# Ten-row loads of an attention backward: other queues, another order, another place

## The chip, the cores and the metric

The kernel runs on one core of a Trainium2 chip. The metric is device time in microseconds (us). Three timed runs of the kernel before gave 902.4, 907.96 and 909.31 us; their median is 907.96. All profile lines come from one profiled execution of the same kernel, which took 901.73 us.

A core has five engines, each working through its own instructions in order: TensorE (PE in the profile, its weight loads PEld), VectorE (DVE), ScalarE (ACT), GpSimd (POOL) and SyncE (SP). In the code they are `T`, `V`, `A`, `G` and `SY`. Any of the last three may issue DMA transfers; the transfers themselves are carried out by 16 DMA engines of the core.

## The reference

The reference is a forward and backward pass of one transformer layer on 2048 rows of 512 elements in bf16, with 32 heads of 16 elements. The layer normalizes, applies a dilated local attention, adds the residual, normalizes again, applies an MLP with 1792 hidden units and gelu, and adds the residual. The outputs are the layer's result and the gradients of x, wqkv, wo, w1, b1, w2 and b2.

The attention looks at eight rows for each row, two apart:

```python
idx = pos[:, None] - off[None, :]          # off = 0, 2, 4, ..., 14
kg = k[:, :, idx_c, :]; vg = v[:, :, idx_c, :]
attn = softmax(where(mask, einsum("bhsd,bhswd->bhsw", q, kg) * scale, -1e9))
o = einsum("bhsw,bhswd->bhsd", attn, vg)
```

The backward of this attention needs three banded sums, one for each of dq, dk and dv: each row of the result is a sum over eight neighbouring rows (of k, of q, and of the gradient of o), each row weighted per head. Those neighbouring rows are what this change loads in another way.

## The kernel before, in words

The program has three stages. The first, to about 250 us, is the attention forward; the second, to about 460 us, is the MLP forward and most of its backward; the third is the attention backward with the weight gradients. q, k, v and the gradient of o (`go_d`) lie in HBM as rows of 512, in `q_d`, `k_d`, `v_d` and `go_d`.

The third stage walks over four chunks of 512 rows, in rounds `for c in range(NC + 2)` (line 869). A round first computes the attention's logit gradients of chunk c (products `pr` on VectorE at line 877 of `got` and the v window `vw`, summed on TensorE at line 883). It then does six bands of 256 rows: two for dv of chunk c-1 (kind "v"), two for dq of chunk c ("q"), two for dk of chunk c-1 ("k"). The rows of the gradient of the input of chunk c-2 (`gln1`, with TensorE's line 845, ScalarE's `gyr` at line 208, GpSimd's `c0` at line 210, VectorE's lines 216 to 221) run beside the logit gradients. So round 1 has bands v0, q1, k0, round 2 has v1, q2, k1, and round 3 has v2, q3, k2; round 0 has only q0, round 4 only v3 and k3.

A band works on a tile R of 128 partitions x 10 rows x 512 elements. Four DMAs (`w4` = 0 to 3, lines 766 to 769) each fill 32 partitions of it. A partition gets ten consecutive rows, 10,240 bytes in one piece; partitions are eight rows apart. R comes from `go_d` for v, from `k_d` for q and from `q_d` for k. VectorE multiplies four rows of R at a time with the coefficients `cf` (line 780, four products for a band), TensorE sums over partitions (line 788), ScalarE copies the result out (line 790), and GpSimd stores it to HBM (line 793).

There are three buffers for R. `load_R` takes the next band of the list `bands`, so two tiles are loaded ahead; at the start of a band (line 774) it asks for the tile two bands later, whose buffer is the one that the previous band has just finished with.

The order of every engine's instructions in this stage is the order in which the Python code issues them (`tc.manual_schedule()`, line 608). `later` puts a piece of work on a list and `slot` runs what is due: with 1 it runs in the very next slot. `slot` then fills TensorE's time with matmuls of the weight gradients from the generator `wgrads`. This filler also issues, on SyncE, the transposing loads `gwm` (line 627) of 256 x 2048 elements, which wait until TensorE has finished with one of two buffers, and the 2 MB loads `gout_r` and `ln2_r` (line 622); its results are copied by ScalarE into `gwst` (line 617) and stored by GpSimd (line 618). SyncE also issues `vw` (line 859), the four-part shifted coefficients `sh` (line 830), `ln1r` (line 175) and the stores of `go_d` (line 238), for which it waits on ScalarE's copy into `tmst` (line 236). Whatever of the filler is left after the bands runs at the end (line 981).

In the built program the DMAs that SyncE and ScalarE issue take turns on eight semaphores, and those of GpSimd on eight others. A DMA therefore waits until the eighth one before it in its group has landed.

Of the kernel before, what the change touches and what calls it, by code (L numbers as in the profile page):

```python
# [27 lines left out]
def _ap(apobj, dims, off=0):  # L28
    return bass.AP(tensor=apobj.tensor, offset=apobj.offset + off, ap=[list(d) for d in dims])
# [7 lines left out]
def kernel(  # L37
# [21 lines left out]
    V, A, T, G, SY = nc.vector, nc.scalar, nc.tensor, nc.gpsimd, nc.sync  # L59
# [4 lines left out]
    S, D = xf.shape  # L64
# [35 lines left out]
    def Y(name):  # L100
        return psY.tile([P, 512], F32, name=name, tag="y")
# [184 lines left out]
    def natural(ps):  # L286
        return ps[:].rearrange("p (d h) -> p h d", h=H)
# [424 lines left out]
    def filler(us):  # L712
        fs["debt"] += us
        while fs["debt"] > 0 and not fs["done"]:
            if fs["gate"] is not None:
                if fs["gate"] not in open_gates:
                    fs["debt"] = 0.0
                    return
                fs["gate"] = None
            x = next(fill, None)  # L720
            if x is None:
                fs["done"] = True
            elif isinstance(x, str):
                fs["gate"] = x
            else:
                fs["debt"] -= x
# [5 lines left out]
    def later(n, cost, fn):  # L732
        pend.append([n, cost, fn])

    def slot(dve_us):
        pe = 0.0
        for x in list(pend):
            x[0] -= 1
            if x[0] <= 0:
                pend.remove(x)  # L740
                x[2]()
                pe += x[1]
        filler(dve_us * RATIO - pe)
# [14 lines left out]
    def load_R():  # L758
        if rpos[0] >= len(bands):
            return  # L760
        kind, c, sc = bands[rpos[0]]
        rpos[0] += 1
        d_t = dict(v=go_d, q=k_d, k=q_d)[kind]
        row0 = c * CH + sc * 256 + (PAD if kind == "q" else 0)
        R = p3.tile([P, 10, 512], BF16, name="R", tag="rows", bufs=3)
        for w4 in range(4):
            r = row0 + (-4 * w4 - 2 if kind == "q" else 4 * w4)
            SY.dma_start(out=R[32 * w4:32 * w4 + 32].rearrange("p a d -> p (a d)"),  # L768
                         in_=_ap(d_t[r:r + 1, :], [[8 * D, 32], [1, 10 * D]]))
        rq.append(R)  # L770

    def band_tile(kind, c, sc, m, cf, gs, sca, after):
        if m == 0:
            load_R()
            bt["R"] = rq.pop(0)
        R = bt["R"]
        pr = p3.tile([P, 2, 4, 512], BF16, name="prb", tag="prod", bufs=3)
        for hf in range(2):
            o = (2 - 2 * hf if kind == "q" else 2 * hf) + 4 * m
            V.tensor_tensor(out=pr[:, hf].rearrange("p j (d h) -> p j d h", h=H),  # L780
                            in0=R[:, o:o + 4, :].rearrange("p j (d h) -> p j d h", h=H),
                            in1=cf[:, hf, sc, 4 * m:4 * m + 4].unsqueeze(2).to_broadcast([P, 4, DH, H]), op=ALU.mult)

        def pe():
            ps = Y("ps_band")
            for hf in range(2):
                for j in range(4):
                    T.matmul(ps[32 * j:32 * j + 32, :], lhsT=S32[:], rhs=pr[:, hf, j, :],  # L788
                             start=(hf == 0), stop=(hf == 1), skip_group_check=True)
            A.activation(out=gs[:, m, :].rearrange("p (h d) -> p h d", d=DH), in_=natural(ps), func=ACT.Copy, scale=sca)  # L790
            if m == 1:
                sel = dict(q=0, k=1, v=2)[kind]
                G.dma_start(out=g3_d[sel][:, 4 * c + 2 * sc:4 * c + 2 * sc + 2, :], in_=gs[:])
                if after:
                    later(1, 1.0, after)
        later(1, 0.7, pe)
        slot(2.45)

    bt = {}
    st3 = [dict() for _ in range(NC + 2)]  # L800
# [62 lines left out]
    load_ln1(0)  # L863
    p3_go(0)
    load_R()
    for _ in range(6):
        slot(0.0)
    load_R()
    for c in range(NC + 2):
        if c >= 2:  # L870
# [39 lines left out]
        def vtile(k):  # L910
            sc, m = k // 2, k % 2
            if m == 0:
                bt["gs"] = p3.tile([P, 2, 512], BF16, name="gks", tag="gks", bufs=2)
            gs = bt["gs"]
            band_tile("v", c - 1, sc, m, cfv, gs, 1.0,
                      lambda gs=gs, sc=sc, c=c: unperm(gs[:], gqkv[c - 1][:, 8:12, :], 4, sc * 256))
# [31 lines left out]
        if c < NC:  # L948
            st3[c]["sh"] = shift(c, attn)
            gqs[c] = []  # L950
            for k in range(4):
                sc, m = k // 2, k % 2
                if m == 0:
                    gqs[c].append(p3.tile([P, 2, 512], BF16, name="gqs", tag="gqs", bufs=2))
                band_tile("q", c, sc, m, cfq, gqs[c][sc], scale, None)
            if c == NC - 1:
                later(2, 0.0, lambda: open_gates.add("q"))
        if c > 0:
            cfk = coefs(p3, shk[:, 0, 0:1], 0, 512)
            for k in range(4):  # L960
                sc, m = k // 2, k % 2
                if m == 0:
                    bt["gs"] = p3.tile([P, 2, 512], BF16, name="gks", tag="gks", bufs=2)
                gs = bt["gs"]
                band_tile("k", c - 1, sc, m, cfk, gs, scale,
                          lambda gs=gs, sc=sc, c=c: unperm(gs[:], gqkv[c - 1][:, 4:8, :], 4, sc * 256))
            if c == NC:
                slot(0.5)
                slot(0.5)
                open_gates.add("k")  # L970
# [49 lines left out]
```

## Time and profile before

| | us |
|---|---|
| median of the timed runs | 907.96 |
| profiled execution | 901.73 |
| its span, first to last instruction | 899.9 |
| PE busy | 659.8 (73%) |
| DVE busy | 531.7 (59%) |
| ACT busy | 335.2 (37%) |
| POOL busy | 126.3 (14%) |
| VectorE's band products, line 780: 96 of 1.219 us | 110.8 |
| time from issue to landing of one of R's DMAs: shortest, middle, longest | 3.7, 7.5, 17.4 |

Of the DMA traffic, 116.55 MB went through the queues of SyncE and ScalarE and 28.87 MB through GpSimd's. Between 500 and 720 us the 16 DMA engines' packets took 84 to 114% of their time (packets overlap, so the share can pass 100%).

The profile names an instruction by its line, engine, operation and tiles as out<-in. Where it gives idle time, the name after the arrow is what ended the wait. A DMA's name, as R<-q_d, says what it writes and reads. "SPq" and "ACTq" are an engine's sequencer, which waits and issues; the time of a DMA line on SPq is that of its issue, not of its transfer.

### The profile page before, as it was taken

To read this page: it belongs to the slowest core of one execution; us is meant where nothing else is said; L and a number is where in the kernel's file an instruction comes from. 1 tells how busy PE (TensorE), PEld (TensorE's weight loads), DVE (VectorE), ACT (ScalarE), POOL (GpSimd) and SP (SyncE) were. 2 spreads that over 40 slices of the span, in tenths; PEclk is the share of its full clock that TensorE was granted. 3 is DMA by queue.
4 is the path that set the end of the run, shared out by engine and by line. 5 is a ranking of instruction groups with operands and counts; after the bars stand their busy time and mean duration, and the time that the engine had idled before them with its cause. 6 is when DMAs were issued, how large, how long until landed. Compare 5 with 4: busy or idle time off the path is not lost. (4 is left out here: it accounts for less than half of the span.)

```text
span 899.9 us, 10402 instructions
## 1 busy us (share of the span) xinstructions
PE 659.8 (73%) x3890; PEld 303.7 (34%) x3948; DVE 531.7 (59%) x774; ACT 335.2 (37%) x497; POOL 126.3 (14%) x213
## 2 busy tenths in 40 slices
PE   4785874655688989988975479779777597862585
PEld 2333332322233433333432133333323356731232
DVE  6786685545876868669476877957965751000000
ACT  2664754436643535634033143343323331110011
POOL 3202112120000201001010002111211122210010
PEclk9996988767899999999996579988986799987798
DMA  8645566584213223324399999999999845532351
GB/s 303 227 114 153 132 184 159 144 188 121 70 60 123 93 89 92 105 71 141 103 243 255 231 241 248 226 222 251 215 233 283 203 139 129 127 111 87 133 201 40
DMA packets 152514, 146.09 MB, mean 162 GB/s; under 512 B 96126, under 2 KB 140751, under 8 KB 147599
## 3 DMA queue, kind: packets, MB, share of 16 engines
q1 hardware_dynamic: 142942, 116.55, 51.5%
q0 software_dynamic: 9520, 28.87, 9.9%
q8 instruction: 31, 0.51, 0.3%
q14 instruction: 21, 0.16, 0.1%
HBM read 72.95 MB, written 47.80 MB: 134 GB/s over the span
## 5 line engine op out<-in xcount | busy, mean ns | idle before, releaser
L780 DVE TENSOR_TENSOR prb<-R,cf 128x2048 bf16<-128x2048 bf16 x96 | 110.8, 1219 | 28.4 <-DMA R<-q_d 22.2
L509 PE MATMUL ps_h<-ln2T,w 128*128 128x512 bf16 x222 | 61.8, 402 | 25.6 <-ACT x L512 22.3
L788 PE MATMUL ps_band<-prb,S 128*32 128x512 bf16 x384 | 42.7, 473 | 48.2 <-DVE prb L780 47.2
L698 PE MATMUL ps_gwq<-gqh,ln_r 128*128 128x512 bf16 x188 | 43.3, 387 | 30.6 <-DMA gqh<-gq_d 26.0
L557 PE MATMUL ps_gg<-goT,w2T 128*128 128x512 bf16 x218 | 53.8, 378 | 11.4 <-DVE gb1p L560 8.6
L661 PE MATMUL ps_gw<-gwm,ln_r 128*128 128x256 bf16 x448 | 54.1, 280 | 8.9 <-ACT gwst L617 8.9
L640 PE MATMUL ps_gw<-gout_r,gwm 128*128 128x512 bf16 x212 | 57.3, 411 | 1.8 <-issue 1.7
L511 ACT ACTIVATE xb<-ps_h,b1c 128x512 bf16<-128x512 f32 x56 | 38.2, 685 | 44.3 <-PE ps_h L509 42.5
L544 PE MATMUL ps_f<-w,gt 128*128 128x512 bf16 x217 | 53.0, 381 | 1.3 <-DVE gt L521 0.9
L618 POOL DMA_DIRECT2D out_dram<-gwst x58 | 31.4, 542 | 150.1 <-ACT gwst L617 143.2
L340 PE MATMUL ps_qkv<-ln1T,wqkv 128*128 128x512 bf16 x185 | 47.3, 392 | 6.8 <-ACT kt L342 3.2
L208 ACT ACTIVATE gyr<-ps_gl,rstd 128x512 bf16<-128x512 f32 x32 | 21.9, 686 | 77.0 <-PE ps_gl L570 24.1
L661 PEld LDWEIGHTS <-ln_r 128*128 128x128 bf16 x448 | 44.1, 100 | 19.0 <-issue 12.9
L790 ACT ACTIVATE gks<-ps_band 128x512 bf16<-128x512 f32 x32 | 19.0, 601 | 69.3 <-PE ps_band L788 57.7
L845 PE MATMUL ps_gl<-wqkvT,gqkvT 128*128 128x512 bf16 x188 | 44.5, 390 | 0.3 <-issue 0.2
L210 POOL TENSOR_SCALAR c<-sg 128x1 f32<-128x1 f32 x32 | 21.9, 686 | 159.8 <-ACT gyr L208 159.6
L509 PEld LDWEIGHTS <-w 128*128 128x128 bf16 x224 | 22.5, 101 | 58.9 <-issue 40.3
L277 DVE TENSOR_TENSOR prb<-R,cf 128x2048 bf16<-128x2048 bf16 x32 | 37.0, 1214 | 7.3 <-DMA R<-v_d 7.3
L512 ACT ACTIVATE x<-ps_h,b1c 128x512 bf16<-128x512 f32 x56 | 37.9, 685 | 7.9 <-DMA ln_d<-ln 5.4
L877 DVE TENSOR_TENSOR pr<-got,vw 128x4096 bf16<-128x4096 bf16 x16 | 35.9, 2285 | 8.1 <-DMA vw<-vf_d 8.1
L243 DVE TENSOR_TENSOR pr<-qt,kt 128x4096 bf16<-128x4096 bf16 x16 | 36.0, 2283 | 7.0 <-ACT qt L342 3.5
L617 ACT ACTIVATE gwst<-ps_gw 128x256 bf16<-128x256 f32 (+1 forms) x42 | 19.1, 455 | 56.1 <-DMA out_dram<-gwst 37.4
(320 smaller groups left out, 1129.0 us busy)
## 6 DMA issues: line engine op xcount, KB each, us to landing
R<-v_d SPq DMA_DIRECT2D x32, 320.0 KB, 5.4
R<-k_d SPq DMA_DIRECT2D x32, 320.0 KB, 7.9
R<-go_d SPq DMA_DIRECT2D x32, 320.0 KB, 7.5
R<-q_d SPq DMA_DIRECT2D x32, 320.0 KB, 7.3
g_d<-gt SPq DMA_DIRECT2D x12, 512.0 KB, 3.3
ln_d<-ln POOLq DMA_DIRECT2D x8, 512.0 KB, 5.7
out_dram<-gwst POOLq DMA_DIRECT2D x30, 128.0 KB, 4.2
w<-in_B_w_dram POOLq DMA_DIRECT2D x2, 1792.0 KB, 11.1
```

Source lines behind the costliest of these rows:

```text
L340: T.matmul(ps[:, gg, :], lhsT=wqkv[:, dc, sel * D + g * P:sel * D + (g + 1) * P], rhs=st_[c]["ln1T"][:, dc, :], start=(dc == 0), stop=(dc ...
L509: T.matmul(ps[:, i, :], lhsT=w1[:, dc, f * P:(f + 1) * P], rhs=ln2T[c][:, dc, :], start=(dc == 0), stop=(dc == DC - 1))
L511: A.activation(out=xb[:, f - f0, :], in_=ps[:, i, :], func=ACT.Identity, bias=b1c[:, f:f + 1])
L512: A.activation(out=x2[:, f - f0, :], in_=ps[:, i, :], func=ACT.Square, bias=b1c[:, f:f + 1])
L544: T.matmul(ps[:], lhsT=gts[f // 4][:, f % 4, j * P:(j + 1) * P], rhs=w2[:, f, :], start=(f == 0), stop=False)
L557: T.matmul(ps[:, i, :], lhsT=w2T[:, dc, f * P:(f + 1) * P], rhs=goT[:, dc, :], start=(dc == 0), stop=(dc == DC - 1))
L640: T.matmul(ps[:], lhsT=gtm[:, t, (f % 2) * P:(f % 2 + 1) * P], rhs=r16[:, t, :], start=(t == 0), stop=(t == NT - 1))
L661: T.matmul(ps[:, 0:256], lhsT=r16[:, t, dc * P:(dc + 1) * P], rhs=ghm[:, t, :], start=(t == 0), stop=(t == NT - 1))
L698: T.matmul(pss[dd][:], lhsT=r16[:, i * HN + t, dc * P:(dc + 1) * P], rhs=hv[i][:, t, :], start=(i == 0 and t == 0), stop=(i == 1 and t == ...
L780: V.tensor_tensor(out=pr[:, hf].rearrange("p j (d h) -> p j d h", h=H), in0=R[:, o:o + 4, :].rearrange("p j (d h) -> p j d h", h=H), in1=c ...
L788: T.matmul(ps[32 * j:32 * j + 32, :], lhsT=S32[:], rhs=pr[:, hf, j, :], start=(hf == 0), stop=(hf == 1), skip_group_check=True)
L845: T.matmul(ps[:], lhsT=gqkv[c][:, b, j * P:(j + 1) * P], rhs=wqkvT[:, b, :], start=(b == 0), stop=(b == 11))
```

## The change

Three things change in `load_R` and one in where it is called. The four DMAs of a tile are issued in the order 0, 2, 1, 3, so that partitions of the lower and the upper half alternate. The q tiles are issued by GpSimd, and their source is described with three dimensions of which the outermost has 8 entries, in place of two with 32 (the same rows to the same places). Of a v tile, parts 0 and 2 stay with SyncE and parts 1 and 3 are issued by ScalarE. The k tiles stay with SyncE. Lastly, `load_R` is called at the end of a band, after its second slot, and no longer at its start; it loads the same tile, two bands ahead, into the same buffer.

```diff
         R = p3.tile([P, 10, 512], BF16, name="R", tag="rows", bufs=3)
-        for w4 in range(4):
+        for w4 in (0, 2, 1, 3):
             r = row0 + (-4 * w4 - 2 if kind == "q" else 4 * w4)
-            SY.dma_start(out=R[32 * w4:32 * w4 + 32].rearrange("p a d -> p (a d)"),
-                         in_=_ap(d_t[r:r + 1, :], [[8 * D, 32], [1, 10 * D]]))
+            dst = R[32 * w4:32 * w4 + 32].rearrange("p a d -> p (a d)")
+            base = d_t[r:r + 1, :]
+            if kind == "q":
+                G.dma_start(out=dst, in_=_ap(base, [[32 * D, 8], [8 * D, 4], [1, 10 * D]]))
+            else:
+                (A if kind == "v" and w4 % 2 else SY).dma_start(out=dst, in_=_ap(base, [[8 * D, 32], [1, 10 * D]]))
         rq.append(R)
 
     def band_tile(kind, c, sc, m, cf, gs, sca, after):
         if m == 0:
-            load_R()
             bt["R"] = rq.pop(0)
@@
         later(1, 0.7, pe)
         slot(2.45)
+        if m == 1:
+            load_R()
```

In the order of the instructions this means: a q tile stands on GpSimd behind the store of the band that has just ended (line 793), a k tile on SyncE behind whatever the two slots of that band have put there, and ScalarE's half of a v tile behind the copies of that band.

## The prediction

> **What bounds the kernel now.** I read the shares and slices first, then the stage table of the attention backward (DVE's bands run from 481 to 730 us), then the waits of VectorE in that stage, then SyncE's and ScalarE's timelines around the longest waits. The waits of VectorE between 480 and 780 us:
>
> ```profile
> DVE junk L216 <- ACT gyr L208: 27.2, 13, 7.9
> DVE prb L780 <- DMA R<-q_d: 22.2, 7, 8.6
> DVE pr L877 <- DMA vw<-vf_d: 7.0, 1, 7.0
> DVE prb L780 <- DMA R<-k_d: 5.7, 3, 3.6
> DVE gx L221 <- DMA out_dram<-gx: 4.1, 1, 4.1
> ```
>
> Columns: total, times, longest. A band costs VectorE 4.63 us (four products of 1.219 us). It waits 27.9 us in all for the ten-row tiles R, none of it for those from go_d, and 7.0 us once for vw. TensorE in the same stage waits for VectorE's products (47.2 us), so both follow the loads. After the bands comes a tail of weight gradients, from about 750 to 890 us, in which no R is loaded; it moves as a block.
>
> SyncE's timeline shows what stands ahead of the late loads (start, length, line, tile):
>
> ```profile
> 469.95 1.93 SPq L768 DMA_DIRECT2D R<-k_d  x4
> 471.92 0.42 SPq L622 DMA_DIRECT2D gout_r<-in_grad_out_dram  x1
> 472.45 20.06 SPq L627 DMA_TRANSPOSE gwm<-g_d  x2
> 492.61 0.55 SPq L859 DMA_DIRECT2D vw<-vf_d  x1
> ...
> 589.60 5.41 SPq L627 DMA_TRANSPOSE gwm<-g_d  x1
> 595.05 2.53 SPq L830 DMA_DIRECT2D sh<-attn  x4
> ...
> 670.05 11.70 SPq L627 DMA_TRANSPOSE gwm<-gh_d  x1
> ```
>
> and VectorE's the two worst waits:
>
> ```profile
> 606.95 4.63 DVE L780 TENSOR_TENSOR prb<-R,cf 128x2048 bf16<-128x2048 bf16 x4 [8.60 <-DMA R<-q_d]
> ...
> 674.47 4.63 DVE L780 TENSOR_TENSOR prb<-R,cf 128x2048 bf16<-128x2048 bf16 x4 [7.37 <-DMA R<-q_d]
> ```
>
> Everything is issued by one engine in order: R for the second q band and gout_r stand ahead of two transposes, and these ahead of vw, which lands at 497.3 us although VectorE is free at 490.5. The first k band of rounds 2 and 3 of the loop waits behind a transpose and four shifts. In the packet records, R's 10,240-byte packets take 0.70 us each, two per DMA engine and DMA; the four DMAs of one R land 1.5 us apart, 6 us a tile, longer than the band that uses it.
>
> **What the Trainium skill says.** "SBUF — State Buffer", section "Can I just issue two DMAs to hit both halves?", says no: one DMA on partition 0 and one on 64 gained only 6% together. The trace agrees: the landing of the third R DMA (first one in the upper half) comes 1.5 us after the second, as within a half. "DMA: Bandwidth & Descriptors", section "Why a DMA increments its semaphore by 16 and not by 1", says that the slowest dimensions of both sides decide how many engines share a DMA, and that from GpSimd a DMA on fewer than 16 takes consecutive engines from a moving cursor. With outer dimension 8 that is eight engines of four rows each, and the next DMA (the other half) the other eight. No DMA before is of that kind. "SBUF — State Buffer", section "Who interferes with whom", expects tensor_tensor not to hold up GpSimd's descriptor writing; the trace agrees as far as it goes: GpSimd's stores take 0.54 us to issue while VectorE multiplies.
>
> **The change part by part**, against the profiled execution (901.73 us, span 899.9); the three timed runs have their median 6.2 us higher, at 907.96, and I apply the difference to that.
>
> *Order 0, 2, 1, 3.* For the k tiles, still on SyncE alone, I take 0 by the 1.5 us spacing above. Below zero at most: full overlap would halve 6 us a tile, 3 us for each late k band. For v, half on ScalarE's queue, any gain is hidden: those tiles have some 20 us of slack.
>
> *q tiles to GpSimd.* Eight tiles x 4 issues x 0.54 us = 17 us of GpSimd, which is 14% busy. If two DMAs run on two groups of engines, a tile takes about 1.5 us of latency and 2 x 1.5 us, 4.5 us from the first issue; if they don't, 7.5. The first two tiles leave SyncE: gout_r is issued 2.0 us earlier and has no R ahead in the rings (R's packets fill 471 to 477.3 us, gout_r's bulk runs 477 to 484). So gout_r, both transposes and vw come about 6.5 us earlier, vw at 490.8 instead of 497.3: **-6.5 us**, with nothing else late there (got is done at 480, products' buffers at 491). If this cover fails (gout_r slower for another reason), the gain is 0.
> The later q tiles now stand behind GpSimd's store of the preceding band, and in rounds 2 and 3 behind a weight-gradient store too (590.55 and 658.40 us). The second q tile of those rounds is then issued at 591.1 and 658.9 and lands 4.5 to 7.5 later; VectorE is ready at 590.8 and 659.4, so waits of 1.05 and 1.08 us become 4 to 8. That is hidden, since the k band after it starts only when its own R lands, at 606.8 and 674.4, and 6.7 us of work stand between. In round 1 the q wait of 3.58 stays (-1 to +1.5): 0.
>
> *k tiles, moved to the band's end.* The buffer is released as before; what counts is what they are moved past on SyncE. The first k tile of rounds 2 and 3 keeps its place (transpose, shifts, tile) but has no q tile in the rings ahead of the transpose, whose landing was 8.7 us against 6.7 in the quiet end of the stage: about -0.75 each, **-1.5 us**. Second k tile of round 1: moved past the go_d stores (534.8 and 535.7 us), lands near 543.7, as before (VectorE started at 544.1): 0. Second k tile of round 3: moved past the transpose of 670.05. Issue near 675 and transfer behind the transpose, landing near 683 instead of 680; the wait of 1.28 grows by **+3.5 us** (0 to +6).
> The gradient rows that follow absorb part: VectorE waits 4.11 us there for an out_dram<-gx store slowed by the 2 MB load of ln2_r and R of the next chunk; a later start meets a quieter DMA. **-2 us** (0 to -4).
>
> *Half the v tiles to ScalarE.* 16 issues x 0.42 us = 6.7 us on an engine about a third busy in this stage (86 of 260 us from 500 to 760), but in order with its evictions. In the built program SyncE's and ScalarE's DMAs share eight semaphores in turn, so each waits for the eighth before it to land (SyncE shows 11 such waits, 11.3 us, at L768 now). Thus ScalarE's last v load of rounds 1 and 2 waits for a gwm transpose, and that of round 3 for ln2_r. Behind it are queued an unpermuting copy and gyr, for which VectorE waits:
>
> ```profile
> 552.70 0.60 ACT L617 ACTIVATE gwst<-ps_gw 128x512 bf16<-128x512 f32 x1 [1.49 <-PE ps_gw L640]
> ...
> 555.91 0.69 ACT L208 ACTIVATE gyr<-ps_gl,rstd 128x512 bf16<-128x512 f32 x1 [1.58 <-PE ps_gl L845]
> ```
>
> ScalarE arrives at 553.3; with 0.9 us of issues and a 1.0 us copy behind, gyr is delayed only if the transpose lands after 554.0. Issued at 547.45 into emptier rings it lands at 554.4 to 556, so gyr slips by 0.4 to 2 us, while TensorE is busy without a break from 553 to 573 and sets the pace of the rows. I take 0 (0 to +20 over the three rounds, below).
>
> Sum: -6.5 - 1.5 + 3.5 - 2 = **-6.5 us**: 895.2 on the profiled execution, 901.5 against the median.
>
> **The rivals.**
> *The loads really speed up.* Two engine groups and a third queue relieve the rings, transposes too, and the R waits go by half: -14 with the -6.5, 887.5 us; all of 27.9 would be 873.6. For it: DMA share is about 1.0 from 500 to 720 us. Against it: the late tiles are k tiles, 22.2 of the 27.9 us, and these keep SyncE, the same engines and the transpose ahead.
> *ScalarE is held (slower).* If the awaited transfers land as late as before (the transpose of 547.45 at 559.27, 11.8 after issue; the one of 615.2 near 627; ln2_r at 700.39), gyr comes 1.9 us after each: 561.2, 628.9, 702.3 instead of 555.9, 624.8, 691.8: +5.3 + 4.1 + 10.5 = +20, less 6.5: 921.5 us. It decides from a landing past 554.0. For it: stores issued on this stage take up to 10 us to land. Against: the v tiles that stood ahead of these transposes no longer do.
> *Nothing moves.* The 6.5 us are won at 490 us and lost at the second k tile and on gyr: 908 us. The change then does in its place what it says, off the path.
>
> **How the numbers follow.** Forecast 0.45 (901.5, spread 895 to 907), speed-up 0.17 (880 to 894), held ScalarE 0.22 (914 to 928), nothing 0.16 (904 to 913). One per cent, about what a measurement of this kernel tells from no change, is 9.1 us: below 898.9 lie the speed-up and four tenths of the forecast, 0.35; above 917 most of the held ScalarE and a little unknown, 0.24; between, 0.41. Leaving out the fast third of the speed-up and the slow half of the held case gives 886 to 922.
>
> **What would show it.** Right: no wait of L877 for vw near 490 us; a wait of 4 to 8 us for R<-k_d in the second q band of rounds 2 and 3, and a smaller one for R<-q_d after it; R<-k_d landing within some 5 us of its first issue. Wrong: gyr's waits growing beyond 27.2 us with ScalarE idle behind a DMA (the third case); R<-q_d waits below 10 us (the speed-up); vw still late; or GpSimd's issues for R much longer than 0.54 us, which would make every q band late.

## The result and the profile after

The changed kernel takes 942.26 us (median of 4 runs, 935.25 to 950.32) against 906.74 for the kernel before on the same chip: a ratio of 1.0371, with an interval from 1.0291 to 1.0451. It is slower by some 35 us; the forecast was 901.5. Ratios leave out executions over 1.5% above the fastest of their kernel, here the profiled one (at the same granted clock as the others, 0.864 against 0.862 to 0.869) and later two of four with the call at the band's start again. The profiled execution took 950.32 us (span 948.5), 8 us over the median, so I use its trace for places and the medians for sizes.

The waits of VectorE between 480 and 820 us of the kernel after (total, times, longest):

```profile
DVE junk L216 <- ACT gyr L208: 39.6, 14, 12.9
DVE prb L783 <- DMA R<-k_d: 38.4, 5, 13.1
DVE prb L783 <- DMA R<-q_d: 22.5, 4, 11.6
```

R<-k_d, the q tiles, went from 5.7 to 38.4 us. R<-q_d stayed where it was in its sum (22.2), but other bands wait now. The wait for gyr is 12 us longer. And TensorE, in the same stretch, has a wait that it did not have before, the second line here:

```profile
PE ps_band L791 <- DVE prb L783: 74.7, 43, 11.5
...
PE ps_gw L640 <- DMA gwm<-g_d: 9.4, 1, 9.4
```

VectorE's timeline shows which bands wait:

```profile
602.14 4.63 DVE L783 TENSOR_TENSOR prb<-R,cf 128x2048 bf16<-128x2048 bf16 x4 [4.63 <-DMA R<-k_d]
614.72 4.63 DVE L783 TENSOR_TENSOR prb<-R,cf 128x2048 bf16<-128x2048 bf16 x4 [7.95 <-DMA R<-k_d]
...
630.87 1.23 DVE L783 TENSOR_TENSOR prb<-R,cf 128x2048 bf16<-128x2048 bf16 x1 [4.50 <-DMA R<-q_d]
...
689.02 4.63 DVE L783 TENSOR_TENSOR prb<-R,cf 128x2048 bf16<-128x2048 bf16 x4 [4.14 <-DMA R<-k_d]
706.79 4.63 DVE L783 TENSOR_TENSOR prb<-R,cf 128x2048 bf16<-128x2048 bf16 x4 [13.14 <-DMA R<-k_d]
...
729.68 3.50 DVE L783 TENSOR_TENSOR prb<-R,cf 128x2048 bf16<-128x2048 bf16 x3 [11.63 <-DMA R<-q_d]
```

602 and 614 are the first and second q band of round 2, 631 its second k band; 689, 707 and 730 are the same three bands of round 3. Two causes stand behind these lines. The first is on GpSimd's timeline:

```profile
591.17 0.54 POOL L796 DMA_DIRECT2D gv_d<-gks  x1 [3.37 <-ACT gks L793]
591.79 1.98 POOL L771 DMA_DIRECT2D R<-k_d  x4
600.12 0.56 POOL L796 DMA_DIRECT2D gv_d<-gks  x1 [6.35 <-ACT gks L793]
601.33 0.55 POOL L618 DMA_DIRECT2D out_dram<-gwst  x1 [0.66 <-ACT gwst L617]
602.00 1.98 POOL L771 DMA_DIRECT2D R<-k_d  x4
```

Each q tile stands behind the store of the band at whose end it is asked for, and that store waits for ScalarE's copy of TensorE's sums. The tile used at 602 is issued at 591.79, that used at 614.7 at 602.00. That is 5.7 and 4.8 us before VectorE is ready for them, at 597.5 and 606.8. In the kernel before, SyncE issued the same two tiles 14.7 and 8.5 us before VectorE was ready, at 586.1 and 590.7:

```profile
571.41 1.99 SPq L768 DMA_DIRECT2D R<-k_d  x4
...
582.22 1.97 SPq L768 DMA_DIRECT2D R<-k_d  x4
```

The second cause is on SyncE's timeline after the change:

```profile
628.58 13.60 SPq L627 DMA_TRANSPOSE gwm<-g_d  x1
642.40 11.60 SPq L773 DMA_DIRECT2D R<-go_d  x4
```

The transposing load of this step, the fourth of the seven that SyncE issues from 540 to 722 us, took 7.9 us to issue before; here it takes 13.6, and lands at 657.9, 29.3 us after its issue (the longest of before was 17.5, behind gout_r; from 540 to 720 us it was 11.8, of those whose landing the trace holds; the last packets of the two others came 10.6 and 13.3 us after issue). During that time ScalarE's halves of two v tiles, issued at 629.02 and 638.45, are in flight. The stretch from 632 to 656 us has a DMA share of 1.16 and moves 118 GB/s: the engines look full and carry about half of what they carried in this stretch before (214 GB/s at a share of 0.94).

### The profile page after: what moved, and what is told of

The parts are those of the page before. It is cut to its first block, busy times and chain, and to the rows that moved or that the text cites. A ratio compares the mean times of both kernels' runs of the same rounds, so it can differ in the third digit from the quotient of the medians.

```text
span 948.5 us, 10511 instructions
## 1 busy us (share of the span) xinstructions
PE 678.8 (72%) x3948; PEld 307.7 (32%) x3948; DVE 532.2 (56%) x774; ACT 335.9 (35%) x497; POOL 142.6 (15%) x245
## 5 line engine op out<-in xcount | busy, mean ns | idle before, releaser
L783 DVE TENSOR_TENSOR prb<-R,cf 128x2048 bf16<-128x2048 bf16 x96 | 111.0, 1219 | 66.1 <-DMA R<-k_d 38.4
L791 PE MATMUL ps_band<-prb,S 128*32 128x512 bf16 x384 | 45.4, 481 | 75.4 <-DVE prb L783 74.7
L509 PE MATMUL ps_h<-ln2T,w 128*128 128x512 bf16 x224 | 64.2, 415 | 23.5 <-ACT x L512 20.4
L640 PE MATMUL ps_gw<-gout_r,gwm 128*128 128x512 bf16 x224 | 63.6, 426 | 9.4 <-DMA gwm<-g_d 9.4
L698 PE MATMUL ps_gwq<-gqh,ln_r 128*128 128x512 bf16 x192 | 44.1, 391 | 30.1 <-DMA gqh<-gq_d 26.0
L850 PE MATMUL ps_gl<-wqkvT,gqkvT 128*128 128x512 bf16 x192 | 46.2, 399 | 0.0
L791 PEld LDWEIGHTS <-S 128*32 128x32 bf16 x384 | 10.0, 98 | 103.8 <-DVE prb L783 68.1
## 6 DMA issues: line engine op xcount, KB each, us to landing
R<-go_d ACTq DMA_DIRECT2D x16, 320.0 KB, 10.4
```

The source lines that it names most:

```text
L509: T.matmul(ps[:, i, :], lhsT=w1[:, dc, f * P:(f + 1) * P], rhs=ln2T[c][:, dc, :], start=(dc == 0), stop=(dc == DC - 1))
L640: T.matmul(ps[:], lhsT=gtm[:, t, (f % 2) * P:(f % 2 + 1) * P], rhs=r16[:, t, :], start=(t == 0), stop=(t == NT - 1))
L698: T.matmul(pss[dd][:], lhsT=r16[:, i * HN + t, dc * P:(dc + 1) * P], rhs=hv[i][:, t, :], start=(i == 0 and t == 0), stop=(i == 1 and t == ...
L850: T.matmul(ps[:], lhsT=gqkv[c][:, b, j * P:(j + 1) * P], rhs=wqkvT[:, b, :], start=(b == 0), stop=(b == 11))
```

## The experiments

Four theories go into the expectations. Theory 1: a transposing load crawls while R's packets run in another engine's queue. Theory 2: a q tile is late because it stands behind the store of the same band on GpSimd. Theory 3: the late call puts tiles behind SyncE's transposes and stores. Theory 4, the slower rival of the prediction: ScalarE is held by its own DMA issues, which wait for a semaphore. Every ratio is to the kernel before, timed on the same chip; the experiments ran on four chips, so compare ratios and not us between them, except where both kernels of a pair ran on one chip.

### One part at a time

The order alone, in the kernel before:

```diff
-        for w4 in range(4):
+        for w4 in (0, 2, 1, 3):
```

> The kernel before with only the order 0, 2, 1, 3 of the four DMAs, all still on SyncE, at the band's start. No theory gives this a part in the 35 us: 907 us, within 4 us of before; the four DMAs of a tile land 1.4 to 1.5 us apart, as they do now, halves or not. If the halves did help, the waits for R<-q_d fall below 15 us.

Measured: 900.3 us, ratio 0.9929 (0.9904 to 0.9954). A miss for all theories, and the fastest kernel of the study that leaves nothing out: it beats both. In the packet records the median time of R's 10,240-byte packets falls from 761 to 702 ns, and the middle spacing between the landings of a tile's DMAs from 1.52 to 1.45 us (v) and 1.54 to 1.41 (q); for the k tiles it stays at 1.42. The waits for R<-q_d go only from 22.2 to 20.5 us; the gain of 3.7 us at the last band is a little here and there.

The late call alone, in the old order, all on SyncE:

```diff
         if m == 0:
-            load_R()
             bt["R"] = rq.pop(0)
@@
         slot(2.45)
+        if m == 1:
+            load_R()
```

> The kernel before with only the call of load_R moved to the band's end, all on SyncE. Theory 1 (transposes and R's packets on different queues slow each other down): everything is still in one queue, so within 5 us of before. Theory 3 (the later place puts tiles behind SyncE's transposes and stores): +8 to +15 us, with waits for R<-k_d in the second q band and for R<-q_d in the second k band.

Measured: 924.5 us, ratio 1.0206 (1.0163 to 1.0249). Theory 3 holds, a little over its range. VectorE's waits for tiles in this kernel, 450 to 800 us:

```profile
DVE prb L785 <- DMA R<-k_d: 28.8, 3, 13.3
DVE prb L785 <- DMA R<-q_d: 23.2, 6, 8.6
```

The first q tile of each round still comes in time (it lands 0.9 to 1.8 us before the band ahead of it ends), the second lands 12.9 and 13.2 us after that point in rounds 2 and 3, and the second k tiles 5.2 to 8.6 us after. Those are behind what the band's second slot has put on SyncE.

The q tiles alone on GpSimd, asked for at the band's start as before:

```diff
-            SY.dma_start(out=R[32 * w4:32 * w4 + 32].rearrange("p a d -> p (a d)"), ...)
+            if kind == "q":
+                G.dma_start(out=dst, in_=_ap(base, [[32 * D, 8], [8 * D, 4], [1, 10 * D]]))
+            else:
+                SY.dma_start(out=dst, in_=_ap(base, [[8 * D, 32], [1, 10 * D]]))
```

> The kernel before with only the q tiles on GpSimd (outer dimension 8, order 0, 2, 1, 3), asked for at the band's start as before. Theory 1 (two queues slow each other down): +10 to +20 us, gwm landing over 12 us after issue where GpSimd's R tiles are in flight. Theory 2 (a q tile is late because it is asked for behind the store of the band just ended): asked for a band earlier in GpSimd's order, it has 5 us more; R<-k_d waits fall to under 15 us from 38, and the time is within 5 us of before or faster by up to 6 (vw comes earlier).

Measured: 903.2 us, ratio 0.9968 (0.9951 to 0.9984); this contains the new order, so GpSimd itself costs some 0.4% on 0.9929. The waits for R<-k_d are 3.5 us in all. GpSimd as the issuer isn't what hurts: theory 2's second half. Theory 1 expected 10 to 20 us here and missed. The packet records show why this run hardly tests it: of the 1,024 R packets in GpSimd's queue only 7 start within 1 us of a hundred or more of a transpose's packets. In the next kernel it is 164 of the 512 in ScalarE's queue.

Parts 1 and 3 of the v tiles alone on ScalarE, at the band's start:

```diff
-            SY.dma_start(out=R[32 * w4:32 * w4 + 32].rearrange("p a d -> p (a d)"), ...)
+            (A if kind == "v" and w4 % 2 else SY).dma_start(out=dst, in_=_ap(base, [[8 * D, 32], [1, 10 * D]]))
```

> The kernel before with only parts 1 and 3 of the v tiles on ScalarE (order 0, 2, 1, 3), asked for at the band's start. Theory 1 (two queues slow each other down): +10 to +20 us, gwm landing some 20 us or more after issue in one of the rounds, TensorE waiting for it at L640. Theory 4 (ScalarE is held by its own DMA issues that wait for a semaphore): about the same sum, but with gwm landing as before and gyr late because ScalarE stands idle before the issue of R<-go_d. Theories 2 and 3: within 4 us of before.

Measured: 935.6 us, ratio 1.0336 (1.0309 to 1.0362), with the new order: +35 us on 900.3, where theory 1 had expected 10 to 20. SyncE's timeline of the order alone, and then of this kernel, at the same step of round 1:

```profile
544.40 6.26 SPq L627 DMA_TRANSPOSE gwm<-g_d  x1
550.77 1.91 SPq L773 DMA_DIRECT2D R<-go_d  x4
563.23 4.42 SPq L627 DMA_TRANSPOSE gwm<-g_d  x1
567.75 0.61 SPq L865 DMA_DIRECT2D vw<-vf_d  x1
```

```profile
546.87 22.06 SPq L627 DMA_TRANSPOSE gwm<-g_d  x1
569.03 1.42 SPq L773 DMA_DIRECT2D R<-go_d  x2
570.54 11.67 SPq L627 DMA_TRANSPOSE gwm<-g_d  x1
582.31 0.61 SPq L865 DMA_DIRECT2D vw<-vf_d  x1
```

SyncE is held in the transpose for 22 us instead of 6, and everything behind it, the other half of the v tile and the vw of the next chunk, moves with it. ScalarE had issued its two parts at 548.7, in 0.81 us, without being held. The transpose lands 31.5 us after issue; TensorE waits for gwm, which it never did in the kernel with the order alone. Its line in the waits of 480 to 780 us, and, from the table by stretches, 552 to 576 us with the order alone and then in this kernel (length, busy of PE, PEld, DVE, ACT, POOL, granted clock, DMA share, GB/s):

```profile
PE ps_gw L640 <- DMA gwm<-g_d: 18.0, 2, 12.0
```

```profile
552.00:576.00 24.00, 22.22 (x142) 8.96 (x140) 20.44 (x29) 6.68 (x13) 5.87 (x10) 0.99 0.89 214
```

```profile
552.00:576.00 24.00, 14.36 (x88) 5.76 (x86) 12.50 (x18) 4.54 (x9) 4.79 (x8) 0.91 1.18 90
```

The transpose's packets of 256 bytes make the difference in the packet records: some 1,500 of them start in the 2 us from 552 of the kernel before, when they run nearly alone, and 120 to 300 in most steps of 2 us here. In this stretch one of them takes 91 ns in the mean, against 21 with the order alone, and 13 of the 64 R packets of ScalarE's queue beside them take 1.3 to 5.5 us, where with the order alone none took more than 0.88. Why the two kinds of packets slow each other down, the records don't show.

### One part undone at a time

> The changed kernel with the order 0, 1, 2, 3 again. The order alone gave 0.9929 of before, some 6 us. If that is a matter of halves, this kernel is 4 to 8 us slower than the changed one (946 to 950); if it was worth something only on SyncE's queue beside the gout_r load, no difference: 942 us.

With the order 0, 1, 2, 3 in the changed kernel: 945.9 us, 1.0437 (1.0397 to 1.0477). It leans to the same 0.7%, but the interval reaches into that of the changed kernel, so it isn't told apart.

> The changed kernel with load_R at the band's start again. If the parts add up as measured one by one (order -6, move +18, q +3, v +35, from 906), 936 to 940 us, with R<-k_d waits below 10 us in place of 38. If ScalarE's v tiles hide what the move costs, no change against the changed kernel: 942 us. Theory 4 expects fewer waits of ScalarE here, since its DMAs come before the band's copies; theory 1 expects the same collapse of the transposes, gwm 20 us or more after issue.

With the call at the band's start again: 945.5 us in the mean of two executions, 1.0427 (1.0376 to 1.0478). The sum of the parts, 936 to 940 us, did not come, though the waits for R<-k_d fell to 3.2 us. The other expectation, no change against the changed kernel (1.0291 to 1.0451), is not contradicted: the intervals overlap. In place of R<-k_d, vw is waited for 17.6 us (longest 15.3), and gwm lands up to 31.3 us after issue, as theory 1 expected. The late call costs nothing that these runs can tell once the transposes crawl.

> The changed kernel with the q tiles on SyncE again. Sum of the parts: 906 - 6 + 18 + 35 = 953; the waits for R<-k_d stay near 30 us, since it is the later place, not GpSimd, that makes them late. If GpSimd's queue is what hurts (theory 2 in its narrow form), 920 us or less.

With the q tiles on SyncE: 930.5 us, 1.0249 (1.0196 to 1.0301); R<-k_d waits 26.0 us. The lateness stays without GpSimd, as expected, but the sum was 23 us too high.

> The changed kernel with all of the v tiles on SyncE again. Sum of the parts: 906 - 6 + 18 + 3 = 921 us, with gwm landing within 12 us of its issue and gyr's waits back to about 32 us. If the collapse comes from GpSimd's R tiles just as well, 935 us or more.

With all of v on SyncE: 941.4 us, 1.0373 (1.0324 to 1.0422), the same as the changed kernel, where 921 was expected. The time is what was expected of transposes that crawl beside GpSimd's R tiles, but that is not what the trace shows. The transposes land within 13.1 us of issue but for two (20.1 behind gout_r, 17.0 beside a q tile of GpSimd in round 3); gyr's waits are at 27.7 us, as before the change. What is left is the lateness, VectorE's waits between 480 and 800 us:

```profile
DVE prb L785 <- DMA R<-k_d: 42.4, 6, 10.3
DVE junk L216 <- ACT gyr L208: 27.7, 13, 9.2
DVE prb L785 <- DMA R<-q_d: 20.7, 4, 8.5
```

So each of two causes gives about the whole loss alone (1.0336 and 1.0373), and both together give it once (1.0371). How VectorE's bands start in four kernels, in us after the kernel before (from the traces):

| band | order | order, q, late call | order, v | all |
|---|---|---|---|---|
| round 1, first q | -1.5 | +2.9 | +4.9 | +3.6 |
| round 1, second k | -3.7 | +10.4 | +1.5 | +11.7 |
| round 2, first v | -3.1 | +9.8 | +9.5 | +11.3 |
| round 2, first q | -3.1 | +14.5 | +12.6 | +16.0 |
| round 2, first k | -3.4 | +13.3 | +12.3 | +14.8 |
| round 2, second k | -3.2 | +18.0 | +15.6 | +17.9 |
| round 3, first v | -3.1 | +18.5 | +23.4 | +30.0 |
| round 3, first q | -3.1 | +24.5 | +23.4 | +34.2 |
| round 3, first k | -3.3 | +26.5 | +23.0 | +38.9 |
| round 4, first v | -2.9 | +29.6 | +25.8 | +44.5 |

With the late call the loss comes at the q and k bands; with v on ScalarE it comes in the stretches between the rounds, where the transposes run. The column of all parts is from an execution 8 us over its kernel's median, and that of the late call from one 6 us under its own: most of the 15 us between their last rows is between these executions, since the medians are 942.3 and 941.4.

### Which cause is it, by itself

For ScalarE's half, the same parts were issued by GpSimd:

```diff
-            (A if kind == "v" and w4 % 2 else SY).dma_start(...)
+            (G if kind == "v" and w4 % 2 else SY).dma_start(...)
```

> As the kernel with only the v tiles split (935.6 us), but parts 1 and 3 are issued by GpSimd and not by ScalarE. Theory 1 (a transpose of SyncE's queue crawls while R's packets run in any other queue): still 925 to 940 us, gwm 20 us or more after issue in two rounds. Theory 4 (ScalarE stands in its DMA issues): 905 us or less, since ScalarE issues no DMA at all. A third reading, that ScalarE's queue alone does this to the transposes: 905 us with gwm within 12 us.

Measured: 927.6 us, ratio 1.0266 (1.0230 to 1.0303). ScalarE issues nothing here, and the transpose at the same step is held just as long, with 103 GB/s in its stretch:

```profile
543.40 22.06 SPq L627 DMA_TRANSPOSE gwm<-g_d  x1
565.56 0.98 SPq L773 DMA_DIRECT2D R<-go_d  x2
```

```profile
549.00:571.00 22.00, 13.20 (x80) 5.08 (x77) 11.26 (x17) 4.43 (x9) 4.97 (x8) 0.88 1.19 103
```

TensorE waits 19.2 us for gwm. Theory 4 falls as the main cause, and so does the reading that ScalarE's queue alone does it. On the order alone (0.9929) GpSimd's half costs 3.4% and ScalarE's 4.1%; where the difference comes from isn't shown.

Then plain loads were put in place of the transposes, with v on SyncE and with v split. Both kernels leave out the transposition, so their weight gradients of w1 and w2 are not those of the reference:

```diff
-        SY.dma_start_transpose(out=t_[:], in_=src)
+        SY.dma_start(out=t_[:].rearrange("p t f -> p (t f)"), in_=src.rearrange("(p a) n -> p (a n)", p=P))
```

> The kernel before with the order 0, 2, 1, 3, and with the transposing loads gwm replaced by plain loads of the same 1 MB into the same tile; it leaves out the transposition, so the weight gradients of w1 and w2 are of untransposed data. It is the base for the next kernel. All theories: 890 to 902 us, R waits a little smaller.

> The same plain loads for gwm (transposition left out), and parts 1 and 3 of the v tiles on ScalarE as in the kernel of 935.6 us. Theory 1 (it is the transposes that collapse): within 8 us of the base with plain loads, throughput never below 150 GB/s where R and gwm run together. Theory 4 (ScalarE held by its DMAs' semaphore waits): +20 us or more against that base, as with transposes.

Measured: 881.9 us (0.9752, 0.9716 to 0.9789) and 885.9 us (0.9796, 0.9754 to 0.9837). Without transposes the split v tiles cost 4.0 us, with them 35.3. The plain loads are issued in 0.34 us, and in the stretch in which the first of round 1 runs beside ScalarE's R packets the engines move 306 GB/s:

```profile
542.60 0.34 SPq L627 DMA_DIRECT2D gwm<-g_d  x1
544.15 0.77 SPq L773 DMA_DIRECT2D R<-go_d  x2
561.52 0.34 SPq L627 DMA_DIRECT2D gwm<-g_d  x1
```

```profile
544.00:556.00 12.00, 12.00 (x78) 4.96 (x77) 9.62 (x10) 4.47 (x8) 2.41 (x5) 1.00 1.03 306
```

ScalarE has the same DMA issues and the same semaphores in this kernel, but the plain loads also land sooner, so it is the run with GpSimd, and not this one, that speaks against theory 4. Nor do these two runs tell the transposition from its packets: a plain load of gwm moves in packets of 8,192 bytes, a transposing one in packets of 256.

For the late tiles, the call was put between start and end: behind the last two products, ahead of the second slot. The q tiles are on GpSimd, v and k on SyncE, as in the kernel of 1.0373.

```diff
-            load_R()
             bt["R"] = rq.pop(0)
@@
+        if m == 1:
+            load_R()
+
         def pe():
             ps = Y("ps_band")
```

> Order 0, 2, 1, 3, q tiles on GpSimd with outer dimension 8, v and k on SyncE, and load_R called between the start and the end of a band: after its last two products are issued and ahead of its second slot, so ahead of the band's own store on GpSimd and of what that slot puts on SyncE. The same with the call behind the slot took 941.4 us. Theory 2 (a q tile is late since the store of the same band stands ahead of it) : 900 to 908 us, waits for R<-k_d below 12 us in place of 42. If it is GpSimd's queue as such, or the DMA rings, 930 us or more.

Measured: 903.4 us, ratio 1.0003 (0.9982 to 1.0024). One slot earlier in the code takes away 3.7% of the kernel before (1.0373 to 1.0003), 33 us. GpSimd's timeline at the step quoted above, and VectorE's waits from 480 to 800 us:

```profile
571.40 1.99 POOL L771 DMA_DIRECT2D R<-k_d  x4
574.77 0.56 POOL L801 DMA_DIRECT2D gv_d<-gks  x1 [1.38 <-ACT gks L798]
575.43 1.97 POOL L771 DMA_DIRECT2D R<-k_d  x4
584.11 0.56 POOL L801 DMA_DIRECT2D gv_d<-gks  x1 [6.71 <-ACT gks L798]
```

```profile
DVE prb L785 <- DMA R<-q_d: 22.1, 4, 7.8
DVE prb L785 <- DMA R<-k_d: 5.6, 3, 2.8
```

The R tile now goes out ahead of the store that waits for ScalarE, 9.6 us before the first q band at 581.0 and 12.2 before the second at 587.6. Theory 2 holds. The call moves for the v and k tiles too, but it is the waits for the q tiles that go, from 42.4 to 5.6 us; those for the k tiles are 20.7 and 22.1, as in the kernel before.

### Whether the lateness needs the transposes

> Order 0, 2, 1, 3 and load_R at the band's end, all on SyncE: the corner missing from the table of the parts. The late place cost 2.1% of before in the old order; if the order is worth its 0.7% here too, 916 to 920 us. If the q tiles' late place costs on GpSimd only (they stood behind the band's store there), the waits for R<-k_d in the first q band stay near 0, and those in the second q band and the second k band (behind SyncE's transposes and stores) make up the loss.

Measured: 925.2 us, ratio 1.0186 (1.0150 to 1.0221), somewhat over the range. So the late call costs 2.6% with the q tiles on SyncE (0.9929 to 1.0186) and 4.0% with them on GpSimd (0.9968 to 1.0373). The bands' waits that this expectation names are read from the kernel with the late call in the old order, above, where they are as it says.

> The changed kernel with all v tiles on SyncE, and gwm by plain loads of the same size (transposition left out). With transposes this was 941.4 us, its base without transposes and without q tiles and late place 881.9. If lateness of the tiles is a cause of its own, +25 to +38 on that base, 907 to 920 us, with waits for R<-k_d still above 30 us. If the loss came from GpSimd's R tiles meeting transposes, within 10 us of the base: below 892 us.

> The changed kernel itself with gwm by plain loads of the same size (transposition left out). If ScalarE's half of the v tiles costs only through transposes, the same time as the kernel without it (the run above), within 6 us. If ScalarE's own waits cost, 15 us or more above it.

Measured: 917.1 us (1.0116, 1.0074 to 1.0158) and 918.8 us (1.0120, 1.0078 to 1.0162). Without a single slow transpose (from 540 us on, gwm lands within 10.4 us of issue, where the trace holds its landing) the late q and k tiles cost 3.6% of the kernel before (0.9752 to 1.0116), 33 us, and ScalarE's half on top costs 1.7, which is nothing that these runs can tell. VectorE's waits, 480 to 800 us, of the first of the two:

```profile
DVE prb L785 <- DMA R<-k_d: 37.2, 6, 7.4
DVE junk L216 <- ACT gyr L208: 27.4, 14, 8.6
DVE prb L785 <- DMA R<-q_d: 17.1, 3, 6.2
```

Lateness is a cause of its own. Why the two causes together don't add is only partly shown. The time that SyncE is held in the issue of the seven transposes between 540 and 722 us, added up from its timelines:

| kernel | us |
|---|---|
| before | 48.3 |
| order | 46.2 |
| order, v on ScalarE | 76.0 |
| order, v on GpSimd | 78.1 |
| order, q, v (early call) | 75.6 |
| order, v, late call | 60.2 |
| order, q, late call | 37.6 |
| all | 56.7 |

With the early call the split v tiles add 30 us to this, with the late call 19, from a lower start. Why it is less isn't shown: the R packets of ScalarE's queue that start within 1 us of a hundred or more of a transpose's go from 223 with the early call to 146 with the late one where the q tiles are on GpSimd, but from 164 to 206 where they are on SyncE. That the rest is hidden in the waits for late tiles is my reading of the two tables, not measured.

## Why the prediction was wrong, step by step

Two terms failed that the sum put at 0: the later q tiles, and half of v on ScalarE. The parts in the order of the prediction:

**Order 0, 2, 1, 3, taken as 0.** Under-sized: it is worth 0.7%, some 6 us. I read from the 1.5 us between landings that halves make no difference. "SBUF — State Buffer", cited there, has 6% for two DMAs on two halves; the packets became 8% shorter (761 to 702 ns in the middle; the 0.70 us that I read for the kernel before was too low). Such a term is to be multiplied by all of the tiles, not called nothing.

**vw 6.5 us earlier.** Right in sign, over-sized. With the q tiles alone on GpSimd, vw landed at 494.4 instead of 497.3, in the changed kernel at 496.2. The first two q tiles left SyncE's queue, but not the DMA engines: in the changed kernel their packets ran until 475.1 us, and the bulk of gout_r's, issued at 470.57, still came only as they ended, from 474 us on (from 477 before).

**A q tile in 4.5 us by two groups of engines, 7.5 at worst.** Wrong. The landings of one tile come 1.41 us apart (466.1, 467.5, 468.9, 470.4), as with all on SyncE in this order, so nothing ran in two halves. From first issue to last landing a q tile took 9.4 to 17.6 us, under the traffic of this stage. GpSimd's issues took 0.49 us each, near the 0.54 assumed.

**The later q tiles, 0.** This is the step that failed for the late call. I named the store of the preceding band for all of them, but priced only the second q tile of rounds 2 and 3, and left the wait of round 1 as it was. Every q tile is asked for behind the band's second slot, so the first one stands behind such a store too, and that waits for ScalarE's copy. By the experiments the late call costs 4.0% with the q tiles on GpSimd, some 37 us. The first q bands of rounds 1 to 3 start 4.5, 4.6 and 4.1 us late in the changed kernel (the profile puts the first down to a transpose of TensorE's, but its tile lands at 525.2, 0.1 us before the start), and round 1's second 8.5. Of the second q bands of rounds 2 and 3 I wrote 4 to 8 us, hidden by the k band after: in round 2 it is 7.95 and hidden (the first k band is 14.8 us behind the kernel before, the first q band 16.0), in round 3 it is 13.14 and hidden in part.

**The k tiles, -1.5, 0, +3.5 and -2.** The second k bands wait 5.9, 4.5 and 11.6 us, against 1.6, 1.3 and 1.3 before. I priced the first at 0, left out that of round 2, and had only the third right in kind. The gradient rows after round 3 absorb 4.8 us (49.3 behind at the last k band of round 3, 44.5 at the next v band), a little more than the 4 that I gave them at most.

**Half of v on ScalarE, 0, or +20 with ScalarE held.** This is the other step that failed. The rival's sign, and gyr's longer waits, which were to show it, came true for another reason, so neither speaks for the rival. gyr waits for TensorE, TensorE for gwm, and gwm for a transfer that crawls. (The profile does put two waits of ScalarE at the start of the stage down to DMAs, 8.5 and 9.4 us until 496.8 and 507.3, but the band that starts then, at 507.25, is 1.1 us earlier than before.) By itself this step costs 35 us, all but 4 of which need the transposes; inside the changed kernel, beside late tiles, it costs nothing more that the runs can tell (1.0373 without it, 1.0371 with it). The page "DMA: Bandwidth & Descriptors", in "Rules for kernel authors", says that a transpose next to ordinary DMAs needs nothing, and in "Issuing engines are not separate DMA queues" that a second issuing engine only saves the time to issue. As far as the rate goes, neither holds here: 90 GB/s pass beside packets of another queue, against 224 in the same stretch of the kernel before, where all of these are in SyncE's queue, and the second engine cost 35 us. The measurement decides.

The sum of -6.5 us thus missed two terms of some 35 us, the late call with the q tiles on GpSimd and the split v tiles. Either alone would have made it slower than the range.

## What to carry to other kernels

A prefetch is as early as the last instruction ahead of it on its issuing engine: before moving one, read that engine's order at the new place and find the wait there, above all a store that waits for the band's own result. Where a queue holds transposing loads, keep other large loads that run at the same time in that same queue; here a free engine that issued half of them made both slow, while the q tiles on GpSimd, whose packets hardly met a transpose's, cost some 0.4%. When each of two parts alone gives the whole loss, undo them one at a time and also alone: undoing only v here (1.0373 in place of 1.0371) would have cleared it wrongly.

## What was not expected of the hardware

A transposing load of 1 MB beside 10,240-byte packets from another queue, ScalarE's or GpSimd's, landed up to 31.5 and 30.1 us after its issue. In the kernel before, from 540 to 720 us, it was 11.8 at most where the trace holds the landing, and 13.3 to the last packet of one where it doesn't. While it runs the DMA share reads 1.16 to 1.19 and only 90 to 118 GB/s pass, and SyncE is held for up to 22.06 us in its issue. A plain load of the same size at the same step of round 1 landed 13.2 us after its issue with the split v tiles and 10.6 without. A high DMA share is thus no proof that the engines move much: it has to be read beside the GB/s.

Alternating the halves of the partitions from one DMA to the next, in one queue, shortened R's packets by 8% and gave 0.7% of the whole kernel.
